# A fused retention-attention and highway layer on one core: 64-row transposes of k and q, balanced row halves, a compact state, two-step feed-forward groups and another order

## The chip, the cores and the metric

One core of a Trainium2 chip runs the whole kernel. The metric is the device time of one execution in microseconds (us), lower is better. Three executions of the kernel before took 109.41, 110.59 and 109.04 us; the median is 109.41 us.

## What is computed

The first stage is a causal linear attention with a decay per head, over 4 batches, 8 heads, 768 positions and 64 channels. The second stage is a highway layer on its output, seen as 3072 tokens of 512 features:

```
for each block of 64 positions:
    intra = (qb @ kb^T * Dmask) @ vb          Dmask[i,j] = lam^(i-j) for i >= j, else 0
    inter = (qb * lam^(pos+1)) @ kv_state
    out   = intra + inter
    kv_state = lam^64 * kv_state + (kb * lam^(63-pos))^T @ vb
x = out as (3072, 512)
H = max(x @ w_h, 0);  T = sigmoid(x @ w_t + b_t)
result = T*H + (1-T)*x
```

## The kernel before, in words

The work is cut into 12 steps n = 0 to 11, three for each batch. A step covers 256 positions of all 8 heads, held as 128 partitions with two positions each (j = 0, 1), and it has two halves b of 128 positions. The decay is put into q (`pow_q`) and v (`pow_v`) when they are cast to bf16, so the state in PSUM (`kv`) only accumulates, and a causal mask `tri` is all that is left of `Dmask`.

Nothing is scheduled by the compiler: the string `PLAN` lists about 520 tokens, and the loop at the end of the function turns them into instructions one after the other. Each engine, and SP's queue of DMA issues, runs its own instructions in the order of the string, so a token that waits holds back every later token of its engine. `@ENG` names the engine of a copy, `=56` the PSUM banks used. The tokens:

- `Lk`, `Lq`, `Lv` (L173): a load of 256 KB, half the heads of one step, from SP's queue. `W` (L177): half of a weight matrix, 512 KB. `ST` (L356, L337): a store of a step's output, 512 KB, or of parts of the last step.
- `CK`, `CQ`, `CV` (L103, L190): cast of k, q, v to bf16, for q and v times the decay; `WC`: cast of weights.
- `TK`, `TQ` (L204): TensorE transposes of k and q, 128 by 128, eight for a step and tensor; `EK`, `EQ`: the copies out of PSUM (L101 on ScalarE, L103 on VectorE).
- `SS` (L216, L221): the scores of one parity e of the heads as 64 by 64 tiles in the rows of e, interleaved with the update of the state by the half b = 1-e, in the other 64 rows. `S` and `U` are scores and states alone. `KE`: copy of the state, 128 by 512 with empty off-diagonal blocks, to bf16.
- `M` (L255): mask of a quarter of the scores on VectorE. `I` (L271): q times the state, four 128 by 128 matmuls for a half. `A` (L281): masked scores times v, 64 by 64 tiles. `D`: copy of the attention output to bf16, which is `xT`, the input of the second stage.
- `F.i.u.w` (L300): eight matmuls, two of the four blocks of 128 output features of `x @ w_h` (w = 0) or `x @ w_t` (w = 1) for the 256 positions of step i. `H` (L305): max(h, 0) - x on VectorE. `G` (L314): the sigmoid on ScalarE, in place in PSUM. `X` (L318): the product, on VectorE.
- `R` (L347, L327): x + product is turned back to tokens in the rows by matmuls with an identity, as 64-row tiles; `E`: the copy out; then `ST`. `Z` (L366): matmuls on zeros that keep TensorE running at the start.

SBUF tiles rotate within pools of the sizes in `BUFS` (five each of kf, qf, vf), so a load waits for the cast that frees its buffer.

Of the kernel before, what the change touches and what calls it, by code (L numbers as in the profile page):

```python
# [17 lines left out]
Lk.0.0 Lv.0.1 Lv.0.0 Lq.0.0 Lk.0.1 Lq.0.1 Lv.1.1 CK.0.0@POOL Lq.1.0 Z.12=0 TK.0.0=0 Lq.1.1 CV.0.0@DVE Lk.1.0  # L18
CQ.0.0@POOL EK.0.0@DVE Lv.1.0 CV.0.1@DVE CK.0.1@ACT Lk.1.1 Z.11=1 TQ.0.0=1 B=2 EQ.0.0@ACT CQ.0.1@POOL W.0.1 W.0.0
Z.6=0 TQ.0.1=3 TK.0.1=4 EQ.0.1@DVE U.0.0 EK.0.1@ACT W.1.1 S.0.0=56 KE.0.0@DVE S.0.1=01 CQ.1.2@POOL W.1.0 M.0.0.1 Z.1=3  # L20
U.0.1 I.0=34 M.0.1.1 KE.0.1@ACT Lk.2.1 M.0.0.0 A.0.1 M.0.1.0 TQ.1.2=0 Lq.2.1 CV.1.2@DVE CK.1.2@ACT EQ.1.2@ACT Lq.2.0
Z.8=1 TK.1.2=1 A.0.0 EK.1.2@DVE Lk.2.0 D.0.0@DVE Z.3=5 SS.1.1=56 WC.0.0.1@ACT WC.0.0.0@POOL M.1.1.0 KE.1.0@ACT
WC.0.1.0@POOL D.0.1@ACT Lv.2.1 WC.0.1.1@DVE Z.4=0 SS.1.0=01 M.1.1.1 I.1=35 KE.1.1@ACT Lv.2.0 F.0.0.0=4 WC.1.1.0@DVE PT
M.1.0.1 Lk.3.1 F.0.1.0=6 M.1.0.0 WC.1.0.0@POOL WC.1.0.1@ACT Lk.3.0 WC.1.1.1@DVE A.1.1 A.1.0 BC F.0.0.1=1 H.0.1 Lq.3.1
D.1.1@ACT H.0.0 D.1.0@ACT F.0.1.1=0 Lq.3.0 CQ.2.2@POOL F.1.0.0=2 Lv.3.0 G.0.1@ACT CK.2.2@DVE F.1.0.1=6 Lv.3.1
G.0.0@ACT X.0.1@DVE TQ.2.2=5 Lq.4.0 X.0.0@DVE TK.2.2=4 EQ.2.2@ACT CV.2.2@POOL F.1.1.0=3 Lq.4.1 EK.2.2@DVE G.1.0@ACT
H.1.0 SS.2.0=01 Lk.4.1 H.1.1 CK.3.2@POOL SS.2.1=54 Lk.4.0 M.2.0.1 F.1.1.1=2 KE.2.0@ACT M.2.1.0 Lv.4.0 TK.3.2=3 M.2.1.1
CQ.3.2@POOL G.1.1@ACT I.2=15 M.2.0.0 Lv.4.1 A.2.1 X.1.0@DVE A.2.0 Lk.5.0 R.0=40 D.2.0@ACT D.2.1@DVE CV.3.2@POOL
TQ.3.2=6 E.0.0@ACT Lk.5.1 F.2.1.1=1 E.0.1@ACT EQ.3.2@DVE Lq.5.1 EK.3.2@ACT X.1.1@DVE F.2.1.0=5 CQ.4.2@POOL Lq.5.0
R.1=40 H.2.1 SS.3.1=62 Lv.5.0 F.2.0.0=3 CK.4.2@POOL KE.3.0@ACT M.3.1.1 Lv.5.1 E.1.1@ACT M.3.1.0 SS.3.0=52 E.1.0@ACT  # L30
H.2.0 Lq.6.0 TQ.4.2=0 KE.3.1@ACT CV.4.2@POOL M.3.0.1 TK.4.2=6 G.2.1@ACT Lq.6.1 F.2.0.1=4 M.3.0.0 EQ.4.2@ACT EK.4.2@DVE
Lv.6.0 I.3=32 A.3.0 CK.5.2@POOL A.3.1 Lk.6.1 SS.4.1=56 D.3.0@ACT D.3.1@DVE TK.5.2=0 KE.4.0@ACT M.4.1.1 Lk.6.0
F.3.0.0=2 G.2.0@ACT CQ.5.2@POOL EK.5.2@DVE Lv.6.1 SS.4.0=36 H.3.0 F.3.0.1=0 Lq.8.0 M.4.0.0 CV.5.2@POOL M.4.0.1
TQ.5.2=2 Lk.9.0 G.3.0@ACT F.3.1.0=3 X.2.1@DVE Lq.7.0 EQ.5.2@ACT X.2.0@DVE F.3.1.1=6 CQ.6.2@POOL M.4.1.0 Lq.7.1
KE.4.1@ACT I.4=14 H.3.1 G.3.1@ACT R.2=25 Lk.8.1 X.3.0@DVE A.4.0 E.2.1@ACT X.3.1@DVE A.4.1 Lk.7.1 SS.5.0=30 E.2.0@ACT
D.4.0@DVE CK.6.2@POOL SS.5.1=56 D.4.1@ACT Lk.7.0 TQ.6.2=2 M.5.0.0 KE.5.0@ACT CV.6.2@POOL TK.6.2=1 M.5.1.1 Lv.7.0
EQ.6.2@ACT F.4.1.0=4 M.5.0.1 Lv.7.1 EK.6.2@ACT F.4.0.0=3 H.4.1 Lk.8.0 M.5.1.0 I.5=62 SS.6.1=01 H.4.0 Lq.8.1 A.5.0
KE.6.0@ACT M.6.1.0 CQ.7.2@POOL R.3=45 Lv.9.1 A.5.1 M.6.1.1 SS.6.0=30 D.5.0@ACT Lv.8.0 F.4.0.1=1 M.6.0.0 D.5.1@ACT
M.6.0.1 Lk.9.1 TQ.7.2=6 G.4.0@ACT CK.7.2@POOL F.5.0.0=3 Lq.10.1 EQ.7.2@ACT F.4.1.1=2 H.5.0 Lk.10.1 E.3.1@ACT X.4.0@DVE
TK.7.2=0 CV.7.2@POOL G.4.1@ACT I.6=63 ST.0 KE.6.1@DVE F.5.0.1=5 X.4.1@DVE Lv.8.1 F.5.1.0=1 G.5.0@ACT CK.8.2@POOL  # L40
EK.7.2@DVE Lq.9.0 A.6.0 E.3.0@ACT H.5.1 A.6.1 SS.7.1=20 Lq.9.1 D.6.0@ACT D.6.1@DVE TK.8.2=4 M.7.1.1 F.6.1.0=1 Lv.9.0
EK.8.2@ACT X.5.0@DVE CK.9.2@POOL F.6.1.1=6 KE.7.0@DVE Lk.10.0 CQ.8.2@POOL H.6.1 R.4=30 SS.7.0=54 Lk.11.1 E.4.0@ACT
F.5.1.1=1 E.4.1@ACT M.7.0.1 G.6.1@ACT ST.4 M.7.1.0 TK.9.2=3 Lq.10.0 M.7.0.0 TQ.8.2=0 G.5.1@ACT CV.8.2@POOL F.6.0.0=4
EQ.8.2@DVE Lk.11.0 KE.7.1@ACT X.5.1@DVE I.7=25 EK.9.2@ACT Lq.11.0 A.7.0 H.6.0 A.7.1 CQ.9.2@POOL SS.8.0=01 X.6.1@DVE
D.7.1@ACT Lv.10.1 SS.8.1=34 M.8.0.1 D.7.0@ACT F.6.0.1=6 KE.8.0@DVE Lq.11.1 CK.10.2@POOL F.7.0.0=5 M.8.1.0 G.6.0@ACT
M.8.1.1 ST.3 TQ.9.2=1 CV.9.2@POOL H.7.0 F.7.1.0=2 EQ.9.2@ACT Lv.10.0 X.6.0@DVE TK.10.2=3 M.8.0.0 ST.1 I.8=45
EK.10.2@ACT CQ.10.2@POOL H.7.1 SS.9.1=61 A.8.1 KE.9.0@ACT M.9.1.0 A.8.0 R.5=02 M.9.1.1 SS.9.0=36 CK.11.2@POOL
E.5.1@DVE F.7.0.1=1 KE.9.1@ACT M.9.0.1 E.5.0@ACT F.7.1.1=2 D.8.0@DVE D.8.1@ACT ST.5 CQ.11.2@POOL M.9.0.0 G.7.0@ACT
Lv.11.1 TK.11.2=6 Lv.11.0 I.9=04 F.8.1.0=5 EK.11.2@ACT ST.2 X.7.0@DVE TQ.10.2=3 G.7.1@ACT H.8.1 CV.10.2@POOL F.8.0.0=1
EQ.10.2@ACT R.6=65 H.8.0 A.9.1 X.7.1@DVE A.9.0 SS.10.1=31 D.9.0@ACT D.9.1@DVE F.8.1.1=2 E.6.1@ACT M.10.1.1 F.9.1.0=0  # L50
E.6.0@DVE G.8.1@ACT M.10.1.0 ST.6 TQ.11.2=4 CV.11.2@POOL KE.10.0@DVE F.9.1.1=5 EQ.11.2@ACT X.8.1@DVE SS.10.0=16
G.9.1@ACT H.9.1 R.7=32 M.10.0.1 KE.10.1@ACT F.8.0.1=4 X.9.1@DVE E.7.0@ACT M.10.0.0 E.7.1@ACT I.10=06 SS.11.0=53
G.8.0@ACT ST.7 A.10.0 M.11.0.0 A.10.1 SS.11.1=21 D.10.1@ACT X.8.0@DVE F.9.0.0=5 KE.11.0@ACT M.11.1.0 D.10.0@ACT
F.9.0.1=6 M.11.0.1 M.11.1.1 F.10.1.0=4 G.9.0@ACT H.9.0 I.11=20 X.9.0@DVE A.11.0 A.11.1 R.8=31 D.11.0@ACT R.9=56
E.8.0@ACT F.10.0.0=2 E.9.0@DVE E.9.1@ACT E.8.1@ACT D.11.1@DVE ST.9 F.10.1.1=3 H.10.0 ST.8 F.10.0.1=6 H.10.1 G.10.1@ACT
F.12.1.1=5 G.10.0@ACT X.10.1@DVE F.11.1.1=1 F.11.1.0=0 G.12.1@ACT X.10.0@DVE F.11.0.1=2 G.11.1@ACT H.11.1 F.12.1.0=4
R.10=36 G.11.0@ACT H.12.1 X.11.1@DVE F.11.0.0=0 E.10.0@ACT X.12.1@DVE F.12.0.1=4 E.10.1@ACT H.11.0 F.12.0.0=1
G.12.0@ACT X.11.0@DVE ST.10 R.11.1.1=5 H.12.0 R.11.0.2=3 E.11.1.1@DVE X.12.0@DVE E.11.0.2@ACT ST.11.1.1 R.11.1.0=0
ST.11.0.2 E.11.1.0@DVE ST.11.1.0
"""  # L60

BUFS = dict(kf=5, qf=5, vf=5, kb=3, qb=2, vs=3, kT=2, qT=2, m=8, xT4=2, th4=2, xT2=3, xT1=2, th2=2, th1=2, hm2=3, hm1=2, tb2=2, tb1=2, ss=4, o=5, oh=2, oq=1)
# [3 lines left out]
def kernel(  # L66
# [74 lines left out]
    kv = ps.tile([128, NP, 128], F32, tag="kv", name="kv", bufs=1)  # L141
# [4 lines left out]

    def groups(n, b):
        return ((n,), b) if n < N - 1 else ((n, b), 0)

    def new(key, shape, dtype=BF16, tag=None):  # L150
        if key not in made:
            tag = tag or key[0]
            made[key] = sb.tile(shape, dtype, tag=tag, name=tag, bufs=BUFS[tag])
        return made[key]

    def bank(key, i, shape, dtype=F32):
        if key not in made:
            made[key] = ps.tile(shape, dtype, tag=f"b{i}", name=f"b{key[0]}", bufs=1)
        return made[key]

    def get(*key):
        return made[key]
# [7 lines left out]
    def load(x, n, p, eng):  # L170
        b, c = divmod(n, NST)
        hs = heads(p)
        (A if eng else nc.sync).dma_start(out=new((x + "f", n), [128, H, J * D], F32)[:, hs],  # L173
                          in_=SRC[x][b, hs, c * 2 * C:(c + 1) * 2 * C, :].rearrange("h (p j) d -> p h (j d)", j=J))

    def load_w(w, g):
        nc.sync.dma_start(out=w_f[w][:, 2 * g:2 * g + 2],  # L177
                          in_=(moe_w_h, moe_w_t)[w][256 * g:256 * g + 256].rearrange("(kc p) m -> p kc m", p=128))

    def cast_w(w, g, i, eng):  # L180
        copy(eng, w_b[w][:, 2 * g + i], w_f[w][:, 2 * g + i])
# [17 lines left out]
    def trans(x, n, p, bk):  # L199
        hs = heads(p)  # L200
        t = bank((x + "tr", n, p), bk[0], [128, (hs.stop - hs.start) // 2, J, C], BF16)
        for i, h in enumerate(range(hs.start, hs.stop, 2)):
            for j in range(J):
                T.transpose(t[:, i, j, :], get(x + "b", n)[:, j, h:h + 2, :], id128)  # L204

    def evac_k(n, p, eng):
        hs = heads(p)
        copy(eng, new(("kT", n), [128, NP, J, C])[:, hs.start // 2:hs.stop // 2], get("ktr", n, p))

    def evac_q(n, p, eng):  # L210
        hs = heads(p)
        copy(eng, new(("qT", n), [128, NP, J, C])[:, hs.start // 2:hs.stop // 2], get("qtr", n, p))


    def score(n, e, hp, j, b):
        T.matmul(get("s", n, e, hp // 2)[half(b), hp % 2, j, :], lhsT=get("kT", n)[half(e), hp, j, half(b)],  # L216
                 rhs=get("qT", n)[half(e), hp, :, half(b)], start=True, stop=True)

    def state(n, b, hp, j, e):
        first = n % NST == 0 and b == 0 and hp == 0 and j == 0  # L220
        T.matmul(kv[half(e), hp, half(e)], lhsT=get("kb", n)[half(b), j, 2 * hp + e, :],  # L221
                 rhs=get("vs", n)[half(b), 2 * hp + e, j, :], start=first, stop=True, skip_group_check=True)

    def scores_state(n, e, bk):
# [194 lines left out]
```

## Time and profile before

| what | us |
|---|---|
| median of three executions | 109.41 |
| profiled execution, first to last instruction (span) | 109.3 |
| TensorE matmuls busy | 99.4 |
| VectorE busy | 82.7 |
| ScalarE busy | 71.9 |
| GpSimd busy | 55.7 |
| first feed-forward matmul starts | 22.09 |

The profile shows one execution. A row of a group or of the timeline names the source line, the engine, the operation, the tile written, the tiles read, shapes and count. `PE` is TensorE's matmuls, `PEld` its weight loads, `DVE` VectorE, `ACT` ScalarE, `POOL` GpSimd, `SPq` the DMA issues of SP. What stands in brackets is the idle time before an instruction and what ended it. [...] what a block of matmuls costs is read from its start to the start of the next block.

### The profile page before, as it was taken

How to read it: one execution, taken by the hardware profiler on the slowest of the kernel's cores; microseconds unless marked ns; L12 is line 12 of the kernel's file. 1: busy time of each engine (PE TensorE's matmuls, PEld its weight loads, DVE VectorE, ACT ScalarE, POOL GpSimd, SP SyncE). 2: the span in 40 equal slices, each digit the busy share in tenths (PEclk: the TensorE clock that was granted, in tenths of full speed). 3: DMA queues.
4: the chain of work that ended last, by engine and by line, in shares of the span. 5: the costliest groups of instructions: out<-in, count | busy, mean ns of one | idle time of the engine just before them, and what ended most of it. 6: DMA issues, size and time to landing. Idle time of an engine off the chain costs nothing.

```text
span 109.3 us, 4968 instructions
## 1 busy us (share of the span) xinstructions
PE 99.4 (91%) x2188; PEld 80.6 (74%) x2190; DVE 82.7 (76%) x140; ACT 71.9 (66%) x129; POOL 55.7 (51%) x46
## 2 busy tenths in 40 slices
PE   4986989899999999999999999998999599999950
PEld 1343654688887878889899889896888478899940
DVE  1241595878998696999977989999858958958960
ACT  3304263787866489499579749975696758776940
POOL 6029420427979858959468296499691600000000
PEclk9999999999999999999999999999999999999999
DMA  0899999999999999989999999599999413207264
GB/s 5 233 304 290 291 366 386 312 290 287 290 266 304 287 250 262 302 228 289 296 300 293 305 341 270 181 346 326 321 333 323 170 69 125 73 6 296 94 233 151
DMA packets 42701, 27.59 MB, mean 252 GB/s; under 512 B 1588, under 2 KB 38712, under 8 KB 42680
## 3 DMA queue, kind: packets, MB, share of 16 engines
q1 hardware_dynamic: 42528, 27.27, 85.1%
q8 instruction: 17, 0.28, 1.2%
q14 instruction: 4, 0.03, 0.1%
q10 hardware_dynamic: 152, 0.01, 0.1%
HBM read 20.98 MB, written 6.29 MB: 249 GB/s over the span
## 4 chain that ended last, share of the span: by engine, by line
PE 61%; DMA 11%; DVE 6%; POOL 5%; ACT 5%; issue 4%; SPq 4%; POOLq 0%; DVEq 0%
PE bt L300 15%; PE bh L300 13%; DMA qf<-in_q_dram 11%; PE bs L216 7%; PE bo L281 5%; PE bx L347 5%; PE bspin L366 4%; PE bqtr L204 4%; DVE m L255 3%; SPq L173 3%; PE bktr L204 3%; POOL qb L190 3%; PE bo L271 3%; ACT qT L101 2%; POOL vs L190 2%
## 5 line engine op out<-in xcount | busy, mean ns | idle before, releaser
L300 PEld LDWEIGHTS <-w_b 128*128 128x128 bf16 x416 | 36.3, 98 | 6.4 <-issue 1.8
L255 DVE TENSOR_TENSOR m<-bs,tri 128x512 bf16<-128x512 f32 x48 | 31.1, 682 | 3.8 <-PE bs L216 3.4
L190 POOL TENSOR_TENSOR qb<-qf,pow_q 128x1024 bf16<-128x1024 f32 (+1 forms) x13 | 23.6, 1813 | 11.2 <-DMA qf<-in_q_dram 10.6
L314 ACT ACTIVATE bt<-bt,bt_col 128x256 f32<-128x256 f32 (+1 forms) x52 | 22.0, 432 | 6.9 <-PE bt L300 4.2
L300 PE MATMUL bt<-xT,w_b 128*128 128x256 bf16 (+1 forms) x208 | 24.5, 265 | 1.3 <-ACT qT L101 1.3
L300 PE MATMUL bh<-xT,w_b 128*128 128x256 bf16 (+1 forms) x208 | 25.0, 265 | 0.2 <-issue 0.2
L190 POOL TENSOR_TENSOR vs<-vf,pow_v 128x1024 bf16<-128x1024 f32 x10 | 19.0, 1904 | 5.0 <-DMA vf<-in_v_dram 4.6
L305 DVE SCALAR_TENSOR_TENSOR hm<-bh,xT 128x512 bf16<-128x512 f32 (+1 forms) x26 | 16.5, 643 | 4.0 <-PE bh L300 2.5
L318 DVE TENSOR_TENSOR th<-bt,hm 128x512 bf16<-128x512 f32 (+1 forms) x26 | 16.5, 643 | 2.1 <-ACT bt L314 2.0
L216 PE MATMUL bs<-qT,kT 64*64 64x128 bf16 x384 | 14.2, 218 | 0.6 <-issue 0.3
L101 ACT ACTIVATE xT<-bo 128x512 bf16<-128x512 f32 x16 | 11.5, 749 | 4.6 <-PE bo L281 4.6
L103 POOL CAST kb<-kf 128x1024 bf16<-128x1024 f32 (+1 forms) x10 | 10.0, 995 | 8.1 <-DMA kf<-in_k_dram 6.8
L101 ACT ACTIVATE ss<-kv 128x512 bf16<-128x512 f32 x15 | 8.9, 595 | 7.3 <-PE bs L216 6.1
L366 PE MATMUL bspin<-blank,id 128*128 128x512 bf16 x43 | 11.8, 416 | 1.6 <-POOL id masks.py:199 1.4
L216 PEld LDWEIGHTS <-kT 64*64 64x64 bf16 x384 | 11.0, 106 | 2.9 <-issue 1.4
L101 ACT ACTIVATE o<-bx 128x512 f32<-128x512 f32 x19 | 10.4, 596 | 1.4 <-PE bx L347 1.3
L101 ACT ACTIVATE qT<-bqtr 128x1024 bf16<-128x1024 bf16 (+1 forms) x10 | 9.8, 980 | 1.8 <-PE bqtr L204 1.8
L281 PE MATMUL bo<-m,vs 64*64 64x128 bf16 x384 | 9.4, 219 | 0.7 <-DVE m L255 0.4
L221 PE MATMUL kv<-vs,kb 64*64 64x64 bf16 x320 | 9.2, 196 | 0.2 <-POOL vs L190 0.2
L366 PEld LDWEIGHTS <-id 128*128 128x128 bf16 x45 | 4.3, 105 | 6.4 <-issue 1.7
L204 PE MATMUL bqtr<-id,qb 128*128 128x128 bf16 x96 | 7.5, 220 | 0.9 <-POOL qb L190 0.9
L281 PEld LDWEIGHTS <-vs 64*64 64x64 bf16 x384 | 6.6, 106 | 2.4 <-issue 1.5
(50 smaller groups left out, 109.1 us busy)
## 6 DMA issues: line engine op xcount, KB each, us to landing
kf<-in_k_dram SPq DMA_DIRECT2D x24, 256.0 KB, 5.5
vf<-in_v_dram SPq DMA_DIRECT2D x24, 256.0 KB, 5.4
qf<-in_q_dram SPq DMA_DIRECT2D x24, 256.0 KB, 5.5
out_dram<-o SPq DMA_DIRECT2D x11, 512.0 KB, 4.7
w_f<-in_moe_w_h_dram SPq DMA_DIRECT2D x2, 512.0 KB, 6.6
w_f<-in_moe_w_t_dram SPq DMA_DIRECT2D x2, 512.0 KB, 8.5
out_dram<-oh SPq DMA_DIRECT2D x2, 128.0 KB, 2.0
out_dram<-oq SPq DMA_DIRECT2D x1, 256.0 KB
```

The lines of the kernel that those rows point to most:

```text
L101: A.activation(dst, src, AF.Copy)
L103: ENG[eng].tensor_copy(dst, src)
L190: ENG[eng].tensor_tensor(dst, in0=get(src, n)[:, heads(p)].rearrange("p h (j d) -> p h j d", j=J), in1=pw[:, n % NST, heads(p), :, None].t ...
L204: T.transpose(t[:, i, j, :], get(x + "b", n)[:, j, h:h + 2, :], id128)
L216: T.matmul(get("s", n, e, hp // 2)[half(b), hp % 2, j, :], lhsT=get("kT", n)[half(e), hp, j, half(b)], rhs=get("qT", n)[half(e), hp, :, ha ...
L255: V.tensor_tensor(new(("m", n, e, u), [128, 2, J, C]), in0=get("s", n, e, u), in1=tri[:, None].to_broadcast([128, 2, J, C]), op=ALU.mult)
L281: T.matmul(get("o", n, b)[half(e), hp, :], lhsT=get("vs", n)[half(b), 2 * hp + e, j, :], rhs=get("m", n, e, u)[half(b), hp % 2, j, :], sta ...
L300: T.matmul(t[:, r, :], lhsT=w_b[w][:, kc, (2 * u + r) * 128:(2 * u + r + 1) * 128], rhs=get("xT", *g)[:, kc, :], start=(kc == 0), stop=(kc ...
L305: V.scalar_tensor_tensor(new(("hm", g, u), [128, 2, z * C], tag=f"hm{z}"), in0=get("h", g, u), scalar=0.0, in1=get("xT", *g)[:, 2 * u:2 * ...
L314: A.activation(dst[:, r, :], src[:, r, :], AF.Sigmoid, bias=bt_col[:, 2 * u + r:2 * u + r + 1])
L318: ENG[eng].tensor_tensor(new(("th", g), [128, NP, z * C], tag=f"th{z}")[:, 2 * u:2 * u + 2, :], in0=get("tt", g, u), in1=get("hm", g, u), ...
L366: T.matmul(t, lhsT=id128, rhs=blank, start=True, stop=True)
```

## The change

- k and q of steps 2 to 11 are transposed by one token `T`: 32 transposes of 64 rows, alternating between the two row halves, each half into a bank of its own; two copies `ET`, one for each half. k and q are kept in one tile `kq`. Steps 0 and 1 keep `TK` and `TQ`, for half the heads at a time.
- Scores and states are dealt out again: `SA` does the first half's state update and half of the scores of e = 0 in row half 0, beside all scores of e = 1 in row half 1; `SB` does the rest of e = 0 beside the second half's state.
- The state is kept as 64 columns for each pair of heads; `KE` copies 128 by 256. `I.n.b` multiplies with it as eight 64 by 64 tiles.
- Feed-forward groups (`GROUPS`): steps 2-3, 4-5, 6-7, 8-9 go together with 512 positions, one block of 128 output features in a token (four matmuls of 512 columns); steps 0, 1, 10 stay alone; step 11 stays as two halves.
- The weights are loaded and cast in halves of their columns (rows of 1 KB) and no longer of their rows (2 KB).
- SBUF buffers are named in the order string too. The order is new: the weights are loaded after all of steps 0 to 3, and of the stores only those of steps 1, 3, 5 and 0 are issued before the last load.

The diff, with the order string cut to the lines around the first feed-forward token and around the last load:

```diff
-CQ.0.0@POOL EK.0.0@DVE Lv.1.0 CV.0.1@DVE CK.0.1@ACT Lk.1.1 Z.11=1 TQ.0.0=1 B=2 EQ.0.0@ACT CQ.0.1@POOL W.0.1 W.0.0
...
+CV.3.2@POOL=3 W.0.1 WC.0.1.0@POOL WC.0.1.1@ACT ET.3.1@DVE A.2.1 A.2.0 D.2.1@DVE=0 SA.3=041 M.3.1.0=5 M.3.1.1=7
+KE.3.0@ACT=2 F.1.1.0=3 H.1.1=0 W.1.1 WC.1.1.0@POOL WC.1.1.1@ACT W.1.0 WC.1.0.1@POOL I.3.1=6 SB.3=2 M.3.0.1=4
...
+X.5.2@DVE=1 Lk.11.1=1 ST.0 Lk.11.0 CK.11.2@POOL=2 T.11=51 ET.11.1@DVE=2 E.6.0@ACT ET.11.0@ACT I.10.0=4 I.10.1=0
...
-    kv = ps.tile([128, NP, 128], F32, tag="kv", name="kv", bufs=1)
+    kv = ps.tile([128, NP, 64], F32, tag="kv", name="kv", bufs=1)
...
-        nc.sync.dma_start(out=w_f[w][:, 2 * g:2 * g + 2],
-                          in_=(moe_w_h, moe_w_t)[w][256 * g:256 * g + 256].rearrange("(kc p) m -> p kc m", p=128))
+        nc.sync.dma_start(out=w_f[w][:, :, 256 * g:256 * g + 256],
+                          in_=(moe_w_h, moe_w_t)[w][:, 256 * g:256 * g + 256].rearrange("(kc p) m -> p kc m", p=128))
...
+    def trans_both(n):
+        for r in range(2):
+            bank(("tr", n, r), [128, 2, NP, J, 64], BF16)
+        for i, x in enumerate("kq"):
+            for hp in range(NP):
+                for j in range(J):
+                    for r in range(2):
+                        T.transpose(get("tr", n, r)[:, i, hp, j, :], get(x + "b", n)[half(r), j, 2 * hp:2 * hp + 2, :], id128[half(r), half(r)])
+
+    def evac_both(n, r, eng):
+        copy(eng, kq(n)[:, :, :, :, half(r)], get("tr", n, r))
...
-        T.matmul(kv[half(e), hp, half(e)], lhsT=get("kb", n)[half(b), j, 2 * hp + e, :],
+        T.matmul(kv[half(e), hp, :], lhsT=get("kb", n)[half(b), j, 2 * hp + e, :],
...
+    def tiles(*rows):
+
+        todo = sorted((sum(w for w, _ in row[:i]), r, i) for r, row in enumerate(rows) for i in range(len(row)))
+        for _, r, i in todo:
+            for go in rows[r][i][1]:
+                go()
+
+    def score_pairs(n, e, hps):
+        return [(56, [lambda hp=hp, j=j, b=b: score(n, e, hp, j, b) for b in range(2)]) for hp in hps for j in range(J)]
+
+    def state_pairs(n, b):
+        return [(32, [lambda hp=hp, j=j, e=e: state(n, b, hp, j, e) for e in range(2)]) for hp in range(NP) for j in range(J)]
+
+    def scores_state_a(n):
+        for e, u in ((0, 0), (1, 0), (1, 1)):
+            bank(("s", n, e, u), [128, 2, J, C])
+        tiles(state_pairs(n, 0) + score_pairs(n, 0, (0, 1)), score_pairs(n, 1, range(NP)))
+
+    def scores_state_b(n):
+        bank(("s", n, 0, 1), [128, 2, J, C])
+        tiles(score_pairs(n, 0, (2, 3)), [] if n % NST == NST - 1 else state_pairs(n, 1))
...
-        copy(eng, new(("ss", n + b, 1 - b), [128, NP, 128]), kv)
+        copy(eng, new(("ss", n + b, 1 - b), [128, NP, 64]), kv)
...
-                    T.matmul(get("o", n, b)[:, hp, :], lhsT=get("ss", n, b)[:, hp, :],
-                             rhs=get("qT", n)[:, hp, :, half(b)],
-                             start=hp == 0, stop=False, skip_group_check=True)
...
+    def inter(n, b):
+        for hp in range(NP):
+            for e in range(2):
+                T.matmul(out_bank(n, b)[half(e), hp, :], lhsT=get("ss", n, b)[half(e), hp, :],
+                         rhs=kq(n)[half(e), 1, hp, :, half(b)], start=o_first(n, b, e), stop=False, skip_group_check=True)
...
+    def block(g, u, w):
+        t = bank(("ht"[w], g, u), [128, len(rows(g, u)), size(g) * C])
+        for r, m in enumerate(rows(g, u)):
             for kc in range(KC):
-                T.matmul(t[:, r, :], lhsT=w_b[w][:, kc, (2 * u + r) * 128:(2 * u + r + 1) * 128],
-                         rhs=get("xT", *g)[:, kc, :], start=(kc == 0), stop=(kc == KC - 1))
+                T.matmul(t[:, r, :], lhsT=w_b[w][:, kc, m * 128:(m + 1) * 128],
+                         rhs=xT(g)[:, kc, :], start=(kc == 0), stop=(kc == KC - 1))
```

## The prediction, made before the result was known

> **What bounds the kernel now.** I read the page first (engine shares, slices, the chain that ended last), then TensorE's timeline, then GpSimd's for the loads.
>
> ```profile
> PE 99.4 (91%) x2188; PEld 80.6 (74%) x2190; DVE 82.7 (76%) x140; ACT 71.9 (66%) x129; POOL 55.7 (51%) x46
> PE   4986989899999999999999999998999599999950
> DVE  1241595878998696999977989999858958958960
> DMA  0899999999999999989999999599999413207264
> PE 61%; DMA 11%; DVE 6%; POOL 5%; ACT 5%; issue 4%; SPq 4%; POOLq 0%; DVEq 0%
> ```
>
> Each slice is 2.7 us. TensorE is full from about 22 us to 104 us, and the DMA engines are full from 3 us to 85 us. So there are two bounds, one behind the other: loads that arrive in order, and TensorE. The chain agrees: TensorE has 61% of the span, and the next share is waiting for loads.
>
> TensorE's timeline gives the price of each token, from start to next start:
>
> ```profile
> 45.67 0.61 PE L204 MATMUL bqtr<-id,qb 128*128 128x128 bf16 x8
> 46.12 1.04 PE L300 MATMUL bh<-xT,w_b 128*128 128x256 bf16 x8
> 46.99 1.04 PE L300 MATMUL bt<-xT,w_b 128*128 128x256 bf16 x8
> 47.87 0.61 PE L271 MATMUL bo<-qT,ss 128*128 128x128 bf16 x8
> 48.41 0.20 PE L347 MATMUL bx<-id,xT 64*128 64x64 bf16 x2
> ...
> 48.98 0.64 PE L281 MATMUL bo<-m,vs 64*64 64x128 bf16 x32
> 49.45 0.22 PE L216 MATMUL bs<-qT,kT 64*64 64x128 bf16 x2
> ```
>
> Eight transposes cost 0.45, an F block 0.87, I of both halves 0.54, R 0.57, A of a step 0.47. R and I hold about 0.10 more than their stream (I: 8 x 0.056 = 0.45; A, same length but no change of tile shape after it, has none). Two SS in a row take 0.86 to 0.87 (29.70 to 30.57), so 0.44 each. I write 0.10 for each change of tile shape. F alone shows the same: 0.97 before an SS, 0.87 before another F.
>
> GpSimd's casts that waited for a load give the pace of the loads:
>
> ```profile
> 12.55 1.90 POOL L190 TENSOR_TENSOR qb<-qf,pow_q 128x1024 bf16<-128x1024 f32 x1 [1.73 <-DMA qf<-in_q_dram]
> 24.32 1.91 POOL L190 TENSOR_TENSOR qb<-qf,pow_q 128x1024 bf16<-128x1024 f32 x1 [2.14 <-DMA qf<-in_q_dram]
> 37.59 1.90 POOL L190 TENSOR_TENSOR vs<-vf,pow_v 128x1024 bf16<-128x1024 f32 x1 [0.30 <-DMA vf<-in_v_dram]
> 84.88 1.90 POOL L190 TENSOR_TENSOR vs<-vf,pow_v 128x1024 bf16<-128x1024 f32 x1 [2.42 <-DMA vf<-in_v_dram]
> ```
>
> By the order string these wait for the 9th, 15th, 30th and 72nd (last) load. From 24.32 to 37.59 fifteen loads take 13.3: 0.885 each. From 12.55 to 24.32, six loads and four weight chunks: (11.8 - 6 x 0.885) / 4 = 1.62 for a chunk.
>
> Before's own time in these terms: first F at 22.1; F, T, SS, I, A, R from there to the last F, counted from the order string, 74.1, with 47 changes of shape 78.8; last F ends at 104.1, so 3.3 of stalls; tail 5.2 to 109.3. The span is 0.1 below the median of 109.41; I forecast both as one.
>
> [...] R's 32 matmuls of 64 columns take 0.47 without the drain, 29 ns for a pair of row halves. [...] The trace: 109 ns at 256 columns (0.87/8), 0.21 us at 512 (eleven zero matmuls in 2.54, less the last one's 0.42, over ten). [...] The trace: 512 KB take 1.62 in 2 KB rows and 1.77 in 512 B rows.
>
> **The change part by part.** All of it in TensorE time, for that sets the end.
>
> T: no row shows 64-row transposes. The nearest is R: 32 matmuls, 64 rows, 64 columns, alternating halves, 0.47. If the halves did not overlap it would be 0.90, what TK and TQ take now. I take 0.47; a step saves 0.43, and ten steps 4.3. T waits for both casts where TK and TQ waited for one each; behind it on TensorE's queue stand SA and the F blocks. The copies keep their size (1024 elements, 1.02 on ScalarE, 0.69 on VectorE); on VectorE they now write runs of 64 elements, and if that halved its speed, 9 x 0.6 = 5 us of VectorE.
>
> SA and SB: in row half 0, eight pairs of states and four of scores; U alone shows a state pair at 31 ns (16 matmuls in 0.44, less the last one's 0.19), a score pair is 55: 0.47; I take 0.48, and SB 0.26. A step: 0.74 against 0.88, 1.7 over twelve. Bounds: 0.70 if all overlaps, 0.98 if the halves hinder each other (+2.9).
>
> I: eight 64 by 64 tiles, two at a time, 4 x 0.056 = 0.225 for a half, as now. It shares its tile shape with A and SA, and the drain after it goes. Upper bound, without overlap, 0.45: +4.5 in all.
>
> F: 4 x 0.216 = 0.87 for the same work: nothing saved on TensorE. ScalarE saves: two sigmoids of 256 at 0.449 become one of 512, 0.67 at the slope of the rows (0.339 at 128, 0.449 at 256): 16 x 0.23 = 3.7. KE at half the width saves some 0.21 of 0.595 on ScalarE. Neither is on the path: ScalarE is two thirds busy. If it were, these 7 us would count.
>
> Weights in 1 KB rows: between 1.62 and 1.77; I take 1.62. All four at 1.77 is +0.6.
>
> The order. From the new string the 24th load (Lv.3.0) stands ahead of W.0.1. I use 0.90 for a load (0.885, and a little for gaps): 12.5 + 15 x 0.90 = 26.0. Then CV.3.2 on GpSimd 1.9, SA.3 with its drain 0.58: F.1.1.0 starts at 28.6, 6.5 later than now. The first weight chunk lands at 27.6 and is cast behind CV.3.2 by 28.5, so it hides. In return steps 0 to 3's attention lies before the first F. From F.1.1.0 to the last F: 44 F x 0.87 = 38.3, 8 short F x 0.45 = 3.6, 8 T 3.8, 8 SA 3.8, 9 SB 2.3, 15 I 3.4, 18 A 4.2, 11 R 5.2: 64.6, and 52 changes of shape 5.2: 69.8, against 78.8.
>
> Do the loads keep up? After the 24th: four chunks to 32.5. T.4 needs four loads more and a CK of 1.04: 37.1; TensorE is there at 28.6 + 8.9 = 37.5. T.9: 35 loads, 65.0 against 64.8. T.10: 41 loads and store 1, 72.1 against 71.6. T.11: the last load after 48 loads and four stores at 1.62 (as 2 KB rows): 82.2, cast 83.3, against 82.2. So TensorE waits about 1.1 at the end of the loads. Stores no longer hold SP: ST.1, 3, 5 and 0 follow their copies by many tokens, and a load's buffer was cast four steps earlier. What comes late then is T.11, and with it all of step 11 (16.2 of TensorE work).
>
> Other stalls: before had 1.1 between 28 and 72 us (0.6 in an A that waited for a mask, 0.5 in an SS); its other 2.7 came from 74 on, around late loads. I keep 1.1. The tail has the same members (max, product, four turns, copy, store): 5.2. The spins before the first F are hidden behind the loads.
>
> Sum: 28.6 + 69.8 + 1.1 + 1.1 + 5.2 = **105.8 us**, 3.2% below 109.3.
>
> **Rivals.**
> *Loads set the end* (0.20). The end by loads is 12.5 + 63p + 13.0 + 1.04 + 16.2 + 0.5 + 5.2 = 48.4 + 63p. At p = 0.95 it is 108.3. For: from 37.59 to 53.59 sixteen loads took 16.0, with SP held by buffers. Against: those holds are gone. No change at 0.965.
> *The row halves do not overlap in T or I* (0.08): +0.43 x 8 = 3.4, or +0.225 x 15 = 3.4: 109.2. Against: R and A overlap. That is the change not doing what it says.
> *VectorE becomes the bound; slower* (0.10). From F.1.1.0 on it has 34 M x 0.62, 44 H and X x 0.62, 8 x 0.37, 5 D x 0.67, 7 ET x 0.63, 3 KE x 0.37, 5 E x 0.63: about 63 us in 69.8, 90%, in one in-order queue. Between 24 and 103 us before it was busy 67.5 of 79, 85%. If it reaches only 81%, F ends at 28.6 + 78 and the kernel at 112. Decides below 82%. For: M, D and H stand between TensorE's blocks and PSUM banks. Against: stretches of the trace hold 97% (48 to 56 us: 7.80 of 8) with TensorE full.
> *Fewer stalls* (0.15): loads at 0.885 and only 0.5 of stalls: 28.4 + 69.8 + 0.5 + 5.2 = 103.9.
>
> **How the numbers follow.** My forecast has 0.47. Range 102.9 to 110.0: the low end takes 0.885 and 0.07 for a change of shape (-1.6); the high end holds the loads at 0.95 and no overlap; its own range without the rivals is 104.5 to 107. About 2% can be told from no change. Faster by over 2% (below 107.2): my case, fewer stalls, a little of the loads: 0.66. Within: the rest of the loads, no overlap: 0.24. Slower: 0.10.
>
> **What would show it.** First F at 28.6; 32 transposes in 0.57; SA at 0.5; last load's cast on GpSimd ending near 83; no stall over 0.5 before 60 us; last F near 100.6. I am wrong if F starts past 31, if T takes 0.9, if SP is held by buffers, or if TensorE waits often for VectorE.

## The result and the profile after

The changed kernel takes 119.16 us (median of four executions, 118.53 to 121.23), the kernel before 109.36 beside it. The ratio is 1.087, 95% interval 1.079 to 1.095: slower, where I forecast 3.2% faster. Medians here are over all executions and ratios over the undisturbed ones (of the four, the one of 121.23 us is left out). The profiled execution took 118.53 us with a span of 116.5; in every execution of which both are known the time is 1.7 to 2.4 above the span.

First the page of the changed kernel, the rows that answer to those of before, with the granted clock and the traffic added; a slice is 2.9 us.

```profile
PE 97.6 (84%) x2296; PEld 65.0 (56%) x2296; DVE 86.1 (74%) x143; ACT 65.1 (56%) x115; POOL 54.6 (47%) x46
...
PE   0299978747859999999999889999999796999930
...
DVE  1100899775864987899999979899799956899740
...
PEclk9999999985555899999999999999999999999995
DMA  1799999999999999999999999300599690000981
GB/s 40 202 307 291 290 290 296 288 308 342 341 293 293 288 291 291 289 285 287 287 298 301 334 304 340 106 6 0 185 280 373 251 344 31 0 0 7 374 292 59
...
PE 64%; DVE 12%; DMA 9%; issue 6%; SPq 3%; ACT 1%; POOLq 1%; ACTq 0%; DVEq 0%
```

Three things are new. TensorE is not full before 34 us. Its clock is at half from 25 to 39 us: four slices at 5, and an 8 on either side. And the DMA engines stand still around 75 to 81 us, before the loads are done. In the chain, "issue" (an engine waits for nothing that the profile shows) has 6% of the span, 7 us, of all engines; 3.3 us of it are TensorE's, in four pieces.

TensorE's timeline, at its start, then at the first feed-forward token, at a T in mid-kernel, at the last T, and at two stalls:

```profile
5.22 0.24 PE L391 MATMUL bbt<-id_f,bt_r 4*128 4x4 f32 x1 [5.22 <-DMA bt_r<-in_moe_b_t_dram]
5.39 6.04 PE L397 MATMUL bspin<-blank,id 128*128 128x512 bf16 x21
11.27 0.39 PE L221 MATMUL bqtr<-id,qb 128*128 128x128 bf16 x4
...
34.01 0.53 PE L241 MATMUL bs<-kq 64*64 64x128 bf16 x9 [1.31 <-issue]
34.47 1.89 PE L335 MATMUL bh<-xT,w_b 128*128 128x256 bf16 x8
36.29 0.42 PE L299 MATMUL bo<-kq,ss 64*64 64x128 bf16 x4
...
51.76 0.41 PE L234 MATMUL btr<-id,kb 64*128 64x64 bf16 x16
52.01 0.40 PE L234 MATMUL btr<-id,qb 64*128 64x64 bf16 x16
52.34 1.04 PE L335 MATMUL bh<-xT,w_b 128*128 128x512 bf16 x4
...
67.40 0.58 PE L309 MATMUL bo<-m,vs 64*64 64x128 bf16 x25 [0.76 <-issue]
...
92.79 0.41 PE L234 MATMUL btr<-id,kb 64*128 64x64 bf16 x16 [0.62 <-POOL kb L117]
...
97.26 0.30 PE L241 MATMUL bs<-kq 64*64 64x128 bf16 x5 [1.06 <-issue]
```

The bias token `B` stands first in the new string, waits 5.22 us for its small load, and holds the spins and the first transposes. F.1.1.0 starts at 34.47 (forecast 28.6) and takes 1.82 at half clock. At 51.76 the price is as forecast: 32 transposes in 0.58.

SP's queue, where I had written "Stores no longer hold SP":

```profile
69.27 0.71 SPq L186 DMA_DIRECT2D qf<-in_q_dram  x1
81.59 0.38 SPq L388 DMA_DIRECT2D out_dram<-o  x1
82.02 1.58 SPq L186 DMA_DIRECT2D vf<-in_v_dram  x1
```

The store at 81.59 is ST.5; from 69.98 on SP waits 11.6 us for its copy.

In spans, 116.5 against 105.8: +5.9 to the first F (34.47 for 28.6), +3.9 from there to the last F's end at 110.36 (75.9 for 72.0, stalls included), +0.9 in the tail (6.1 for 5.2).

### The profile page after: what moved, and what is told of

It reads as the page before. It is cut to its first block, busy times and chain, and to the rows that moved or that the text cites. A ratio compares the mean times of both kernels' runs of the same rounds, so it can differ in the third digit from the quotient of the medians.

```text
span 116.5 us, 5174 instructions
## 1 busy us (share of the span) xinstructions
PE 97.6 (84%) x2296; PEld 65.0 (56%) x2296; DVE 86.1 (74%) x143; ACT 65.1 (56%) x115; POOL 54.6 (47%) x46
## 3 DMA queue, kind: packets, MB, share of 16 engines
q1 hardware_dynamic: 43552, 27.27, 82.2%
## 4 chain that ended last, share of the span: by engine, by line
PE 64%; DVE 12%; DMA 9%; issue 6%; SPq 3%; ACT 1%; POOLq 1%; ACTq 0%; DVEq 0%
PE bt L335 16%; PE bh L335 14%; PE bspin L397 7%; PE bo L309 6%; PE bs L241 6%; DVE m L283 5%; DMA kf<-in_k_dram 5%; PE bx L379 4%; PE btr L234 3%; PE bo L299 3%; DMA bt_r<-in_moe_b_t_dram 3%; PE kv L246 2%; SPq L186 2%; DVE th L349 1%; DVE hm L339 1%
## 5 line engine op out<-in xcount | busy, mean ns | idle before, releaser
L335 PEld LDWEIGHTS <-w_b 128*128 128x128 bf16 x288 | 24.5, 100 | 14.6 <-issue 0.5
L204 POOL TENSOR_TENSOR vs<-vf,pow_v 128x1024 bf16<-128x1024 f32 (+1 forms) x12 | 21.3, 1776 | 18.9 <-DMA qf<-in_q_dram 10.7
L335 PE MATMUL bt<-xT,w_b 128*128 128x512 bf16 (+2 forms) x144 | 25.0, 316 | 0.0
L335 PE MATMUL bh<-xT,w_b 128*128 128x512 bf16 (+2 forms) x144 | 24.7, 316 | 0.0
L346 ACT ACTIVATE bt<-bt,bt_col 128x512 f32<-128x512 f32 (+2 forms) x36 | 18.4, 520 | 10.3 <-PE bt L335 9.3
L241 PE MATMUL bs<-kq 64*64 64x128 bf16 x384 | 16.4, 234 | 2.7 <-issue 2.4
L241 PEld LDWEIGHTS <-kq 64*64 64x64 bf16 x384 | 12.1, 115 | 3.2 <-issue 2.8
L115 ACT ACTIVATE kq<-btr 128x1024 bf16<-128x1024 bf16 x11 | 11.1, 1022 | 4.6 <-PE btr L234 4.5
L246 PEld LDWEIGHTS <-kb 64*64 64x64 bf16 x320 | 8.8, 114 | 2.9 <-issue 1.3
L117 DVE CAST xT<-bo 128x512 bf16<-128x512 f32 x9 | 6.4, 726 | 1.7 <-PE bo L309 1.6
```

Of the source, the lines that this page charges most:

```text
L115: A.activation(dst, src, AF.Copy)
L117: ENG[eng].tensor_copy(dst, src)
L204: ENG[eng].tensor_tensor(dst, in0=get(src, n)[:, heads(p)].rearrange("p h (j d) -> p h j d", j=J), in1=pw[:, n % NST, heads(p), :, None].t ...
L246: T.matmul(kv[half(e), hp, :], lhsT=get("kb", n)[half(b), j, 2 * hp + e, :], rhs=get("vs", n)[half(b), 2 * hp + e, j, :], start=first, sto ...
L335: T.matmul(t[:, r, :], lhsT=w_b[w][:, kc, m * 128:(m + 1) * 128], rhs=xT(g)[:, kc, :], start=(kc == 0), stop=(kc == KC - 1))
L346: A.activation(get("tt", g, u)[:, r, :], t[:, r, :], AF.Sigmoid, bias=bt_col[:, m:m + 1])
```

## The experiments

My theories on reading this: a late start (the bias), half clock, the held SP, and TensorE's instructions arriving late. The last, the fetch theory of the expectations, came from the trace. The page counts 18 packets of 16 KB (0.29 MB) on a queue "instruction" for 2296 matmuls, one for about 128 of them and their weight loads (2296/18 is 127.6), and TensorE's "issue" pieces end 2.3 to 3 us after such a packet begins. That they are waits for instructions is the theory; the profile names no cause. The rival to all of them is that the prices of the new tokens only hold in isolation; the price theory of the expectations is that these prices hold and set the time.

**The bias moved behind the first spins** (changed kernel otherwise).

```diff
-... Lk.0.0=0 Lk.0.1 B=0 CQ.0.1@POOL=0 ... Z.21=2 TQ.0.1=1 EQ.0.1@DVE=0
+... Lk.0.0=0 Lk.0.1 CQ.0.1@POOL=0 ... Z.21=2 TQ.0.1=1 B=0 EQ.0.1@DVE=0
```

> The changed kernel with the bias transpose moved behind the first 21 spins and the first transposes of q. Start theory (the bias transpose, first in TensorE's queue, waits for its load until 5.2 us and holds the spins and the first transposes, which then come at 11.3): first transposes near 7.5, first scores near 10.6 instead of 14.9, first F near 30 instead of 34.5, TensorE's clock full again, time down by 4 to 6 us. Clock theory (TensorE runs out of work while the loads of steps 2 and 3 arrive, whatever the first spins do): first transposes near 7.5, but the clock halves all the same between 20 and 36 us, first F above 33, time down by less than 2 us.

117.02 us, ratio to before 1.067 [1.058, 1.076]. First transposes at 8.74, first F at 30.96, still at half clock (1.82). Of the 9.8 us lost, 2.1 are the bias.

**The last loads moved ahead of ST.5** (changed kernel otherwise).

```diff
-... ST.5 Lv.11.0 F.5.0.0=3 ... Lq.11.0 ... Lk.11.1=1 ST.0 Lk.11.0 CK.11.2@POOL=2
+... Lv.11.0 Lq.11.0 Lk.11.1=1 Lk.11.0 ST.5 F.5.0.0=3 ... ST.0 CK.11.2@POOL=2
```

> The changed kernel with the four last loads moved ahead of the store of step 5 in SP's queue. Store theory (SP stands at that store from 70 to 81.6 us, the DMA engines idle, and the last loads land 8 us late): no DMA gap, the last cast of k ends near 80 instead of 92.7, T.11 no longer waits; as TensorE itself is at T.11 only at 92.2, the time falls by 0.6 to 1.5 us. If the gap set more than that (through the buffers and banks that came free late), the time falls by 3 us or more.

120.04 us, 1.096 [1.086, 1.105]: no gain. The last T no longer waits 0.6 us, but the "issue" pieces are 4.5 us in all (2.4 and 2.1) where they were 3.3. The hold is real and was not what set the end.

**Both moves together.**

> Both edits. If start and stores are two independent losses, the fall is the sum of the two; if an earlier start makes TensorE reach the loads' gap sooner, it is more than the sum, by up to 4 us: start theory 110 to 113 us; clock theory 115 to 118.

118.24 us, 1.071 [1.064, 1.079]: the bias alone, within the intervals.

**The bias moved first in the kernel before.**

```diff
-Lk.0.0 Lv.0.1 ... Lq.1.0 Z.12=0 TK.0.0=0 ... TQ.0.0=1 B=2 EQ.0.0@ACT
+Lk.0.0 Lv.0.1 ... Lq.1.0 B=2 Z.12=0 TK.0.0=0 ... TQ.0.0=1 EQ.0.0@ACT
```

> The kernel before with its bias transpose moved to the front of TensorE's queue, ahead of the first 12 spins, as the changed kernel has it. Start theory: the spins start at 5.2 instead of 1.4, the first transposes slip by 2 to 4 us and the time rises by 2 to 4 us. Clock theory: the time rises by less than 1 us, since loads pace the start.

111.82 us, 1.023 [1.017, 1.029]: 2.5 us, about what it costs in the changed kernel, from the other side.

**Spins in the idle stretches of steps 2 and 3** (on top of the bias moved).

```diff
-M.1.0.1=7 A.1.1 ... T.2=61 ET.2.1@ACT=2
+M.1.0.1=7 Z.2=3 A.1.1 ... T.2=61 Z.8=3 ET.2.1@ACT=2
```

> The changed order with the bias behind the first spins (117.0 us), and three spins of zero matmuls added before steps 2 and 3 (two of 512 columns ahead of A.1.1, eight after T.2), where TensorE idled for late loads and the granted clock fell to half. Clock theory: the clock stays full through the first feed-forward blocks, F.1.1.0 takes 0.87 and not 1.82, the time is 115 to 116. Rival, the clock falls for another reason: the dip stays, 117 or more, for the spins add up to 2 us of work.

116.07 us, 1.048 [1.037, 1.060], hardly apart from the 117.0. TensorE's timeline of this kernel:

```profile
31.26 0.26 PE L246 MATMUL kv<-vs,kb 64*64 64x64 bf16 x2 [1.62 <-issue]
...
31.93 1.89 PE L335 MATMUL bh<-xT,w_b 128*128 128x256 bf16 x8
```

The clock is now full from 24.0 to 27.5 us (1.00; with the bias alone it was 0.50 from 24.1 to 27.6), but 2.3 us of stall ahead of and inside SA.3, 1.62 of it on "issue", come right before F.1.1.0, and from 31.1 us the clock is down again. The expectation of a full clock failed. In this kernel the half clock follows a stall, and work ahead of the stall did not cure it.

**T undone** (bias moved; k and q of steps 2 to 11 by 16 transposes of 128 rows again, at T's places).

```diff
-T.4=20 ET.4.0@DVE=1 ... ET.4.1@ACT
+TK.4.2=2 TQ.4.2=0 EK.4.2@DVE=1 ... EQ.4.2@ACT
```

> The changed order with the bias behind the first spins (117.0 us), with steps 2 to 11 transposed by 128 rows again (16 matmuls for k and q where T has 32), everything else kept. Price theory, what my forecast counts on: T saves 0.43 a step, so 10 steps cost 3 to 4 us more: 120 to 121. Fetch theory: the 32 short matmuls outrun the fetch of instructions, TensorE's stalls with no cause shown go from about 3 us to below 1.5, and the time stays within 1 us of 117.

113.54 us, 1.036 [1.029, 1.043]: 3.5 us *faster* than with T, although TensorE has 8 x 0.33 = 2.6 more to do from the first F on. It is past both expectations, on the fetch theory's side in time, but not in stalls, which that theory had below 1.5 us. Its page and its timeline:

```profile
PE   4999779358869999999999999996969999999960
...
PEclk9999999999999999999999999999999999999996
```

```profile
29.83 1.05 PE L336 MATMUL bh<-xT,w_b 128*128 128x256 bf16 x8
...
32.42 0.24 PE L242 MATMUL bs<-kq 64*64 64x128 bf16 x1 [1.09 <-issue]
```

F.1.1.0 starts at 29.83 at full clock, and the stalls on "issue" are 3.0 us in all, against 4.3 with T. So the largest gain of my sum, 4.3 us, has the wrong sign here. Where the 3.5 us lie is shown only in part. The two profiled executions, 113.95 us and with T 115.55, are closer than the medians: the first F starts 1.1 us earlier without T, from there to the end of the last F it takes 76.8 us against 76.3, and the tail is 1.0 shorter. Half clock is not the whole of it: the page shows none here before the tail, but the three other executions of this kernel, with a mean clock of 0.97, took 113.2 to 113.7 us, no longer than this one. And the edit lets the first copy start when half of the transposes are done, where T's copies wait for all 32; that is not separated.

**T alone in the kernel before** (ten of eleven steps, old order).

```diff
-TQ.2.2=5 ... TK.2.2=4 EQ.2.2@ACT ... EK.2.2@DVE
+T.2=45 ET.2.0@ACT ... ET.2.1@DVE
```

> The kernel before in its old order, with T and its two copies in ten of the eleven steps (all but 7), and a third buffer for the transposed tile; nothing else of the change. Price theory: ten steps save 0.43 us each of a TensorE that is full, less what T waits for the later of two casts: 105 to 106.5. Fetch theory: the saving is eaten by stalls that no wait explains and by late casts: 108.5 to 110, and such stalls together above 2 us where the kernel before has 0.7.

114.11 us, 1.049 [1.043, 1.055]: 5 us slower, at full clock, worse than both theories had it, and so with a cost that neither names. T itself takes 0.57 there too.

**The same, with 16 transposes of 128 rows inside T.** Places, banks and copies' sizes stay.

```diff
-    for r in range(2):
-        T.transpose(get("tr", n, r)[:, i, hp, j, :], get(x + "b", n)[half(r), j, 2 * hp:2 * hp + 2, :], id128[half(r), half(r)])
+    T.transpose(get("tr", n, i)[:, hp, j, :], get(x + "b", n)[:, j, 2 * hp:2 * hp + 2, :], id128)
```

> The kernel before with T at the same ten places, banks and copies as when it was tried alone (114.1 us), but with 16 transposes of 128 rows, k into one bank and q into the other, for the 32 of 64 rows. What is left of T is its place: both casts first, then both copies. Price theory: 0.33 us a step more than with 64 rows, 117 to 117.5. Fetch theory: 160 instructions pairs fewer, the stalls with no cause shown fall from 1.9 us to below 1, and the time is 112 to 114. If the place is the whole cost of T alone, it stays above 114 with waits for copies and masks as the main idle time.

112.46 us, 1.032 [1.027, 1.037]: 1.6 us faster than with 64 rows, with 3.3 more of TensorE work. The stalls on "issue" of both kernels, each in the list of TensorE's waits (in total, times, longest), first with 64 rows:

```profile
PE kv L236 <- issue: 0.8, 1, 0.8
PE bo L296 <- issue: 0.5, 1, 0.5
PE bx L362 <- issue: 0.5, 1, 0.5
```

then with 128:

```profile
PE bo L295 <- issue: 0.4, 1, 0.4
```

1.9 us become 0.4. That is 1.5 of about 4.9 us that full rows win back (1.6 of time, and the 3.3 of work); TensorE's waits for copies of kq fall as well, from 2.7 to 1.9, since k's copy need not wait for q's transposes. The other 2.6 are not shown. What stays, 3.3 us over before, belongs to T's place and the one tile for k and q. The waits name copies of kq (1.9 us), but I haven't split this further.

**The fetch by itself.** To the kernel before I added 400 matmuls on zeros, 64 rows by 64 columns, alternating row halves, ahead of R.0:

```diff
+        for _ in range(200):
+            for i in range(2):
+                T.matmul(t[i][:, :64], lhsT=id128[half(i), :], rhs=blank[half(i), :64], start=True, stop=True)
```

> The kernel before with 400 matmuls of 64 rows and 64 columns on zeros, alternating the row halves, put ahead of R.0 near 35 us. Stream theory: 29 ns a pair as in R, 5.8 us without a gap. Fetch theory: each 128 matmuls use up a block of 16 KB of instructions, which takes about 2.7 us to come: about 8.4 us, with gaps of 0.5 to 1 us each some 128 matmuls that no wait explains.

They took 12.4 us, more than the fetch theory's 8.4: runs of 128 matmuls, which I call blocks, begin 5.1 us apart (38.43 and 43.52), and not the 2.7 that I had put on a block. TensorE's timeline:

```profile
33.78 2.33 PE L372 MATMUL bn<-blank,id 64*128 64x64 bf16 x148
38.43 2.04 PE L372 MATMUL bn<-blank,id 64*128 64x64 bf16 x128 [2.31 <-issue]
43.52 2.60 PE L372 MATMUL bn<-blank,id 64*128 64x64 bf16 x124 [3.06 <-issue]
46.14 0.24 PE L347 MATMUL bx<-id,xT 64*128 64x64 bf16 x2
...
48.35 0.24 PE L347 MATMUL bx<-id,xT 64*128 64x64 bf16 x2 [1.91 <-issue]
```

128 matmuls run in 2.0 us (16 ns each), then nothing runs until 5.1 us after the block began; the next period is 4.8. The clock falls to half within the third block (0.50 from 46 to 50 us). The same 400 ahead of R.8, where the DMA engines are 2% busy:

> The 400 narrow matmuls on zeros moved to stand ahead of R.8 near 100 us, where the loads have ended (ahead of R.0, with the loads running, they took 12.4 us, 128 of them in each 5.1 us). If blocks of instructions come late only because they share the DMA engines with the loads: 5.8 to 8 us. If a block takes its time in any case: 11 to 13 us again.

```profile
98.45 2.04 PE L372 MATMUL bn<-blank,id 64*128 64x64 bf16 x128 [1.83 <-issue]
102.18 1.92 PE L372 MATMUL bn<-blank,id 64*128 64x64 bf16 x120 [1.69 <-issue]
```

A block each 3.7 us (98.45 to 102.18), 1.4 less than under the loads, and a stall of 1.7 stays without them. All 400 take 9.9 us, between my two values. And with each 16 matmuls holding two of 512 columns, ahead of R.0 again:

```diff
+        for _ in range(25):
+            for i in range(14):
+                T.matmul(t[i % 2][:, :64], lhsT=id128[half(i % 2), :], rhs=blank[half(i % 2), :64], start=True, stop=True)
+            for i in range(2):
+                T.matmul(t[i], lhsT=id128, rhs=blank, start=True, stop=True)
```

> 400 matmuls on zeros ahead of R.0 as in the first narrow test, but of each 16, two have 512 columns and 128 rows: 128 of them now take about 6 us by their streams and shape changes, where 128 narrow ones took 2.0 and then 3.1 of stall. If a block of 128 matmuls is fetched while the one before it runs, and takes 5.1 us to come: no stall inside, 17 to 20 us in all. If each block costs its 3 us of stall whatever runs: 26 us or more.

```profile
33.72 0.38 PE L372 MATMUL bn<-blank,id 64*128 64x64 bf16 x14
34.02 0.60 PE L374 MATMUL bn<-blank,id 128*128 128x512 bf16 x2
34.56 0.38 PE L372 MATMUL bn<-blank,id 64*128 64x64 bf16 x14
...
54.38 0.61 PE L374 MATMUL bn<-blank,id 128*128 128x512 bf16 x2
54.92 0.31 PE L347 MATMUL bx<-id,xT 64*128 64x64 bf16 x2
```

400 matmuls in 21.2 us, a little above the 17 to 20 expected, 6.8 for 128, and not one stall. So what TensorE stalls on passes beside the work: no stall shows where a block lasts 6.8 us, and where a block's work lasts 2.0, TensorE stands idle for the rest of 5.1. That the limit is at about 5 us is my estimate from the two; no run here has a pace in between.

## Why the prediction was wrong, step by step

*The token prices* held. T took 0.58 at 51.76 us, SA with its change of shape 0.60 (47.84 to 48.44), an F block 0.87 (0.97 before a change; this 0.10 is all that "drain" stands for in my forecast), with no doubling in T or I; that rival is out. The prices leave out the stalls on "issue", 3.3 us here.

*The sum of TensorE work, 69.8, with 2.2 of stalls* is the step that failed in kind: it put stalls on "issue", and the clock, at nothing. From F.1.1.0 to the last F the string has 1792 matmuls, 14.0 blocks of 128. In my 72.0 us that is 5.1 us a block on average, just the 5.1 at which blocks followed each other under the loads in the narrow test, and the F blocks of 512 columns (0.22 us a matmul) leave much less for the stretches between them. By that measure, an estimate, the forecast had no room before the first stall. The kernel before has 1924 matmuls from its first F to its last in 82.2 us, 5.5 a block, and 0.7 us of stalls on "issue"; the changed one took 75.9 us, 5.4 a block, with 2.0 of them, and 1.3 more just ahead of its first F. With up to 2.2 of half clock (below), 0.6 at T.11 and 0.5 in a wait for VectorE, 5.3 us in all where I had 2.2, most of the 3.9 over the forecast are named. (My account of before's stalls did not add up: 1.1 and 2.7 are 3.8, the sum leaves 3.3; only the 1.1 went into the forecast.) I read "issue 4%" in before's chain and did not ask what it was.

*T saves 4.3 us* is the largest term that failed, and it is shown wrong twice: taking it out of the changed kernel gains 3.5 us, and in the kernel before it costs 1.6 against full rows at the same places. It takes 0.58 us in place of 0.90 by issuing 32 matmuls for 16, in kernels that stall on "issue" without T too (3.0 us in the changed one with T undone, 0.8 in before); these stalls are 1.3 and 1.5 us of it, and the rest of the loss is open. That its copies are slower is out: 682 ns on VectorE and 1022 on ScalarE, as before.

*First F at 28.6.* It came at 34.47. The loads are a small part of that. The cast of v that SA.3 waits for ended at 29.08, where I had 27.9:

```profile
27.18 1.90 POOL L204 TENSOR_TENSOR vs<-vf,pow_v 128x1024 bf16<-128x1024 f32 x1
```

The other 4.7 us TensorE was late itself. "The spins before the first F are hidden behind the loads" failed: I left out the wait of `B`, the first instruction in TensorE's queue (2.1 us of the total, confirmed at 2.5 in the kernel before). The rest is late casts (two of VectorE's 128x512 scalings took 1.53 and 1.56 us where before's took 0.69), half clock and a 1.31 us stall on "issue". Not separated further: the spins changed the time too little. With `B` moved and T undone, SA.3 starts at 29.23, right behind that cast (29.19), and the first F comes at 29.83.

*Half clock* stood nowhere in my sum. F.1.1.0 alone loses 0.85 by it (1.82, where 0.97 is due before a change of shape); the clock stays at half to 38.8 us, 4.4 us from the first F on, so I estimate at most 2.2 lost there. In three runs it follows stretches with stalls: in the changed kernel a wait of 1.83 us that ends at 24.37, with the spins the 2.3 us ahead of and inside SA.3, in the first narrow test, in its third block, the "issue" stalls of 2.31 and 3.06.

*"Stores no longer hold SP"* was wrong: I compared places in the string, not times. SP runs ahead of the loads, so it reached ST.5 at 70 us, and R.5 stood at 79.7. T.11 waited 0.6 for it. Moving the store brought nothing, so its price stays below what the runs can tell.

*Rivals.* "Slower" was right for a reason I had not named: VectorE is 74% busy, and TensorE's waits for it are 5.3 us in all, all but 0.5 of them ahead of the first F, where they are part of the late start. Loads did not set the end: with the last ones moved forward the time did not fall.

*The two executions.* I put before's span of 109.3 equal to a time of 109.41; executions of 109.2 to 109.4 us have spans of 107.1 to 107.5. So the one I priced took some 2 us longer than these, and I left out 1.9 around it; the two cancel in the level.

The 9.8 us by what the runs show: bias 2.1, T 3.5, together 5.6, down to 113.5. It is still 4.2 above before. Its profile shows 3.0 of stalls on "issue" against before's 0.8, so perhaps 2.2 of it; no run takes these out. Seen another way, its first F starts 7.9 us later than before's (29.83 for 21.92; the 22.09 of my table is where the chain takes that block up), and to the end of the last F it makes up only 5.4 (76.8 us against 82.2). My sum without T's saving, 74.6, would have made up most of it. What costs the rest isn't settled. No version here beats the kernel before.

## What to carry to other kernels

Count instructions as a resource beside time: for each 128 consecutive matmuls add up their stream time, and compare it with the pace of the narrow blocks here, 3.7 us with the DMA engines 2% busy and 5.1 with them full. My estimate from blocks of 2.0 us of work, which stalled, and of 6.8, which did not, is that TensorE waits for the difference. By the same count I expect splitting a matmul into row halves to pay only where wide matmuls stand around it; no run here shows such a gain. For a wait in an in-order queue compare times, not places in the string (SP stood 11.6 us at ST.5), and look at the very first instruction of each queue (`B` waited 5.22 us, with the spins behind it).

## What the hardware showed that was not expected

- Short matmuls ran in blocks of 128 with idle time between them: with 16 ns matmuls a block each 5.1 us with the DMA engines full, 3.7 with them 2% busy, 3.1 and 1.7 us of it stall. A packet of the queue "instruction" falls between two blocks' starts: with full engines it begins 2.5 us after the block before it starts to run (41.0 for 38.43), with idle ones 1.0 (99.5 for 98.45); from packet to first matmul it is 2.5 and 2.7 us. At a pace of 6.8 us a block no stall shows. That the stalls are waits for these packets is my reading of the times.
- The clock fell to half though TensorE worked on. In the changed kernel the granted clock falls at 25.2 us and is back at 38.8. Busy time by windows (TensorE, its weight loads, VectorE, ScalarE, GpSimd, then granted clock, DMA share and GB/s):

```profile
18.36:21.77 3.41, 3.31 (x86) 1.86 (x87) 2.65 (x4) 1.67 (x4) 3.01 (x2) 1.00 1.17 290
21.78:25.19 3.41, 1.58 (x90) 1.38 (x89) 2.69 (x6) 0.11 (x1) 1.90 (x1) 1.00 1.12 292
25.19:38.84 13.65, 10.67 (x244) 8.48 (x237) 9.31 (x16) 5.82 (x9) 9.54 (x9) 0.50 1.13 316
```

  The longest wait of TensorE after its start, 1.83 us, ends 0.8 us before the fall, and in the second row's 3.41 us it was busy for 1.58. Busy time over a longer stretch does not tell the kernels apart: from 24 to 32 us TensorE was busy for 5.96 us at a mean clock of 0.57 in the changed kernel, and for 5.51 at 1.00 with T undone. What makes the clock fall is not shown.
- VectorE's f32 scaling of 128x512 took 0.68 to 1.56 us in one kernel, with nothing changed in the instruction. The two long ones began while GpSimd ran a scaling of its own, and ended 0.56 and 0.55 us after it; the two that began before GpSimd's took 0.68 and 0.71. No experiment separates this.

```profile
14.46 1.25 POOL L204 TENSOR_TENSOR vs<-vf,pow_v 128x512 bf16<-128x512 f32 x1 [0.19 <-DMA vf<-in_v_dram]
14.74 1.53 DVE L204 TENSOR_TENSOR qb<-qf,pow_q 128x512 bf16<-128x512 f32 x1
18.02 1.90 POOL L204 TENSOR_TENSOR qb<-qf,pow_q 128x1024 bf16<-128x1024 f32 x1 [2.31 <-DMA qf<-in_q_dram]
18.91 1.56 DVE L204 TENSOR_TENSOR vs<-vf,pow_v 128x512 bf16<-128x512 f32 x1
```
